# One search step for the order of a fused attention and MoE kernel: all engines, loads, paces and PSUM banks

## The chip, the core and the metric

The kernel runs on one core of one Trainium2 chip. The metric is the device time of one execution in microseconds; three runs were shown for the kernel before. TensorE is called PE, ScalarE ACT, VectorE DVE, GpSimd POOL and SyncE SP, as the profile names them.

## The reference

```python
batch, n_heads, seq, head_dim = (8, 8, 1152, 64)     # q, k, v in float32
q_pool = q.reshape(B, H, S // 2, 2, D).mean(axis=3)  # pairs of query rows are averaged
scores = scale * np.matmul(q_pool, k.transpose(0, 1, 3, 2))
attn = softmax(scores)                               # with the row's maximum and sum
x = matmul(attn, v).transpose(0, 2, 1, 3).reshape(4608, 512)
h1 = x @ w1; h2 = x @ w2                             # 512 -> 1024
out = np.maximum(h1, h2) @ w_out                     # 1024 -> 512
```

So there are 8 batches of 8 heads, 576 pooled queries against 1152 keys each, and then a two-layer block on 4608 tokens whose middle is the larger of two products.

## The kernel before, in words

**Work.** Two heads of one batch make a *pair*; there are 32 pairs. For each, SP loads q, k and v (576 KB each, three raw buffers of each kind, used in turn), POOL casts them to bf16 (q by adding its two rows), and k and q are turned so that the head dimension lies on the partitions: k by a DMA transpose from SP (`ktrans`, L475; from pair 5 on), q by eight 32x32-block transposes on DVE (`qtrans_dve`, L485). The first five pairs are turned on PE. PE makes the scores in groups of 512 columns for both heads (`scores`, L302, 324 groups, each over two PSUM banks), ACT takes their exponential to bf16 (`exps`, L317, 336 instructions), and PE multiplies with v, in which a column of ones gives the sums (`av_jobs`, L621 for 128-row chunks and L636 for the 64-row rests). DVE divides (L651, L654), and a DMA transpose from SP (L703) puts the result into `xT`.

The MoE block uses max(h1, h2) = relu(x(w1 - w2)) + x w2. POOL makes w1 - w2 once (`w_diff`), PE makes w2 times w_out once (the two w jobs), then *h jobs* (L760) give the relu part by token blocks of 128 to 512 columns (evacuated by DVE at L771 or ACT at L775), and *p jobs* (L803) add relu part times w_out and x times w2 w_out for 256 tokens (evacuated at L809 or L812, stored from SP at L829 or L835). The last tokens are three *z jobs* (L846). An h or p job runs its contraction on 64-row halves in two turns, with the halves swapped in the second; the second turn's first matmul waits for the first turn's results (`fence=True`).

**Order.** Every engine works through one list in order, and all five lists come from one string of letters: each letter issues the next piece of its kind (S scores, E an exponential, A an AV part, 0 to 3 a part of an open MoE job, 4 to 7 and 8, 9, +, - the evacuation of such a job by DVE or ACT, a an AV division step, k, q, v the casts, r a q transpose, t and x the DMA transposes, l the next load of LOADS, o and z stores, F a filler matmul). BANKS gives each opened piece its PSUM bank. Waits follow from the data that a piece reads and overwrites. So the string decides on what stands behind what on an engine, and on SP's queue in particular loads, DMA transposes and stores stand in one order.

**Pacing.** From the 40th exponential on, a load of q, k or v waits besides for the exponential that was issued two before its place in the string (`pace`):

```python
def pace():
    g = done[0] - PACE
    return [f"E{g}"] if PACE and g >= PACE_FROM else []
```

Of the kernel before, what the change touches and what calls it, by code (L numbers as in the profile page):

```python
# [116 lines left out]
def bass_funnel_attn__then__act_maxout2_kernel(  # L117
# [11 lines left out]
    E = moe_w_out.shape[1]  # L129
    SQ = S // 2  # L130
    NT = S // P
    HP = P // 2
    QU = SQ // HP
# [14 lines left out]
    K0 = (0, 2, 4, 6, 9)  # L148
# [12 lines left out]
    BEHIND = ()  # L161
    FILL = 28
    FILLS = 16
    PACE = 2
    PACE_FROM = 40
    FOUR = 1
    LOADS = (
# [14 lines left out]
    )  # L182
    MOE = (
        "wwhhhhpphhhhpphhhhhhhhpphhhhpphhhhphhhhpphhhhphhhhphhhhpphhhhhhhhhphphh"
    )
    BANKS = (
        "0124605424023623462032424660232342630240624702402064202420472042646264246024604640164604264126402406"
        "0240260240246304260346204040640606062061262062062402740264062402406402640642704260202402402406401640"
        "6460462056204620462046042164206204620620426026402602602602604604614646046046024604604204620420642040"
        "6406406742064264264206520640260462620620162062046206240620206204230642042042424126426046046045620642"  # L190
        "6024062046206206206206412640246056046206404024024026423236042642042626260262626426454526420642064206"
        "2454"
    )

    ctx = ExitStack()
    with ctx:
# [146 lines left out]
        def load_k(i, lo=0, hi=NT, eng="SP"):  # L343
            b, h0, s = i // NHP, 2 * (i % NHP), i % 3
            old, name = behind() if eng == "SP" else ([], [])
            op(eng, lambda e: e.dma_start(  # L346
                kraw[s][:, :, lo:hi, :].rearrange("p h t d -> p h (t d)"),
                k[b, h0:h0 + 2, :, :].rearrange("h (p t) d -> p h (t d)", t=NT)[
                    :, :, lo * D:hi * D]),
                after=([f"kraw0.{c}" for c in K0] if s == 0 and hi - lo == NT else []) + pace() + old,  # L350
                w=([f"kraw0.{lo}"] if hi - lo < NT else [f"kraw{s}"]) + name,
                dma=f"d_kp{lo}" if hi - lo < NT else f"d_k{s}",
                cost=0.2 * (hi - lo) + 0.03 if hi - lo < NT else 1.45 + 0.6 * (i == 1), tag=("L", "k", i))

        def load_q(i, lo=0, hi=QU, eng="SP"):
            b, h0, s = i // NHP, 2 * (i % NHP), i % 3
            old, name = behind() if eng == "SP" else ([], [])
# [5 lines left out]
                after=(["qraw0.0", "qraw0.4"] if s == 0 and hi - lo == QU else []) + pace() + old,  # L363
# [561 lines left out]
        def step(c):  # L925
# [5 lines left out]
            elif c == "E":  # L931
                g, go = exp_at.pop(0)
                go()
                done[0] = g
            elif c in lines or c in "0123":
                if c not in opened:
                    job = (moe if c in "0123" else lines[c]).pop(0)
# [19 lines left out]
                 "m": ("Z", 0), "4": ("0", 0), "5": ("1", 0), "6": ("2", 0), "7": ("3", 0),  # L957
                 "8": ("0", 1), "9": ("1", 1), "+": ("2", 1), "-": ("3", 1)}
        for c in (
            "luFFlulllfyKQklgfbSkKEFlgFKSgESyFFlKEFgQSbESlFkSFEFFKlEySFSgESlqFFEFQlSbEFkSQElbKvSEgSlESceAAEATcESA"  # L960
            "EAhlkSaSEaASclEKAEglSAEcSAElvSaTaEhElTcSAESlAhAEScAElSSAcEAAlAqESa0a00aE0la0ScAE0SldQEaa00bSd0lEXSj0"
            "00ESvTl0h0E00eS4SlEAAkAEAlSa1ad1E1S1SEl1q1S1E1Kl1g1qE1S1SE1lQkrAEbArSdtAErArSE11avlEa1S5AElSdArESSrA"
            "dArEArSAEkAlaAaSEaAdatAESaXadjXEjSjSEXq0jl00jE0S0qr0E0lSr01rE11e41Sl1E1Sk1r10Er005St0ESv00r0ESSr0rvE"
            "lA4AAEASqalSaEAArAErAlSrSEEaAeaAArxAErSSaAEaAklrAAErS1at1ak1E1r0Sr0xE0r0Sr11E1rS1r0E050Sl0E0q0SrS0tE"
            "r01r10Er0eS0r0E0r0Skr0lE0r1S0r0E0rlSv0r1E14S11El1S1oSE1oAAEASAkEAaAlaSAEtAvSa1aE1SxS11ES111E1111ES11"
            "l1ESq5AAEAlSrSoEAroArAESrkSArEAaAalAEAaAaSvaaEtaSSrXEqArAjAEAjSrle00Ea0aS0rSE0lr0vSr0E1r01rlE114S11E"
            "1S1rSEA5AlvAEASr0E0ta0Eva0SrSE00xe00SE4AAkAESSlAEAaAaAEAlSa1aE1Sx000E0Sk11E0lS11E11S50qlE00tS00ESer0"
            "0rSE00rS0rE00r00Er0l0qSrSE0r01l1r0E14S11E1l1SroSE1r1o11roSErAoArAtEkArAAaaAArq1ESaa1E1Sx001r001E1r0S"
            "1rE0l001rS141E1rS1r1ES5AAEvAAroSSrvoESAlAAEvAaAaAlEAaAkaSa000SaEt0a000011114Ee111S111115E1S111Xl5EvS"
            "j00j0ESl0qSE0000SEl4AAAEArSSaEAaArAlqEArS1a1taE11rSESrE1e1xrS1r1EA5AAEASla0kaE0Sr00rSEq0l0r0SEr0ArAl"  # L970
            "E4SAAESr11aE1a1Srx1ESr11r1SEt5qAAAEArSe0aE0a0Slr0SEkr0S0r0E0lrS0r0E0r0Sl0rE0000ES0S0Er0tArAEArArS0aE"
            "0aq0Srx10Er1S14k1E1S11EroS1rSo1E1oAAoEvAAS1vElSAAlEAvAaSa1ESalAaAAEASa1aE1taS1rXvE1rS1j11Ej1eSrl11rE"
            "11qrSS5EAlAAkEAroS0a0oEa0S0rS0ErAAlAEASa0a0E0l0S4x00E0qSE0r00E0trSA4eAEAArS1a1Ea1k1Sr11ESr1lSr1E5AAA"
            "lEArS1a1Ea11Srx00E10S1l1E1S500tE0Sq0rS0Er00r0e0ESr00rSEl0kr00r0E0rS0l0ES00SE0A4AAEAAaAoaAoASaoSqaE11"
            "x11SESkr11t1rE11rE11rE1SrS1E1r11r1SEr11S1E1S11E1A5AEvAASoSvESlAAoAEvAaAaAElAaAa0Sa0a0E0taS00r0000E04"
            "e0Sx000r0E11141vS1x1E11r100500Sr11qE1Sr01lr110E1rS050E0Sl0r0E0SS0l0E0S0r0EArAArEAArlAkaAaArSE0etEa0a"
            "S0r0SE0rxS0rq0EA4AAEASkao1aE11o1SSE11lS11EA5AAElASa1aE1Sx0r00E0rS1rt0E0er0Sr0E1S4111ESl1r0q0E500S0lE"
            "0SrS0r0EA4lAAEAAAaaAASa1aESlk1Sx1r1ES1r11Ert11r11Er1qSSr1E1rArAEvAS1E11klS11El11vS1E1S1lvA5ESAAEAoAa"
            "oSaSESaAtaArAEArq00Ea0aSa00rExSv0r00ErS0xe0r0E0rSSr0kl0E0S00E0Sl00E0S00El0A4AEAAAaoSaSEoArAtArE00Ea0"
            "0aeS00rxE1111r00qS411E1111151S1k1E1r1Sl00500ESr000SrEl0A4AAEArSla1aE1S1S1EAAAEAlSa1aE1tSrS1rq1E1r1x1"  # L980
            "1rESSre11Er11rSk1Elr11S1E11Sl1E1A5AAEASaoSaEAoAAoEAoSa0a0tEq00rSESr0E00rx00k040E0AArvAArSrSvElArArAE"
            "AvaAaAAaAaSaSaE00a001x14E11S11E1x11Sv511E100S1SE0r1t11r0ES0500E0eSr00Er00SrSE0r00r0SEr0S00E0S00E0004"
            "0E00S0E0oS00oSE4AAAEAAaAaAeAAaEAaAAxAaAaAASa0aES0x00SE1000E0S411E1S11E111500S0E00S11E1S11E1S10E50S00"
            "E0S10E0Se10E00S00E0S00E0S00E10S41E11S11EoS11o1E1oSSo1E1AAEAAAaAaAAAaAaAxAAAAAaAaAAaAa1a1a1a11X1j11j1"
            "11111900001111111150000111o080110091o110000008101110191101000018111009101110000080101111191100000001"
            "001111910000000011111111110001000800110000o008001o11o00010181111Z9ZZZZZoZZoZZZZZZmZZZZzzZZZZZZZZZZmZ"
            "ZZZZZZzZzmzz"
        ):
            step(c)
# [52 lines left out]
```

## Time and profile before

| | us |
|---|---|
| three runs | 357.15, 358.04, 360.08 |
| median | 358.04 |
| span of the profiled execution | 356.4 |
| TensorE busy | 346.0 (97%) |
| ScalarE busy | 313.8 (88%) |
| VectorE busy | 230.1 (65%) |
| GpSimd busy | 151.4 (42%) |

For the profiled execution the page gives its span alone, the time from the first to the last instruction; the median of the three runs lies 1.64 us above it. Matmuls overlap in TensorE, so sums of their durations exceed the time that they take; start-to-start distances are used where that matters. The granted TensorE clock of the profiled execution is 0.999. Lines such as L302 are those of the kernel's file.

### The profile page before, as it was taken

The page shows a single profiled execution, that of the slowest core. Times are in us where ns is not written, and L with a number is a line of the kernel's source. Part 1 is how long each engine was busy: PE and PEld are TensorE (multiplying, and loading weights), DVE is VectorE, ACT ScalarE, POOL GpSimd, SP SyncE. Part 2 cuts the span into 40 slices and gives each one's busy share as a digit, 9 for nine tenths or more (in the row PEclk, how much of TensorE's full clock was granted, in tenths as well). Part 3 has the DMA queues.
Part 4 walks back from the last instruction along what each step waited for, and adds up shares of the span by engine and source line. Part 5 has one row for each costly group of instructions (what it writes and reads, how often), then busy time and mean ns, then how long its engine had stood idle before and what let it go on. Part 6 is the DMA issues. An engine that isn't in the chain of part 4 may idle for free.

```text
span 356.4 us, 13757 instructions
## 1 busy us (share of the span) xinstructions
PE 346.0 (97%) x6178; PEld 218.5 (61%) x6178; DVE 230.1 (65%) x472; ACT 313.8 (88%) x354; POOL 151.4 (42%) x136
## 2 busy tenths in 40 slices
PE   7889999999899999999999999999999999999996
PEld 5556665656564675656666576556576757448753
DVE  2587589974966867985887677785586875414001
ACT  5999999999999899999999989989999796992431
POOL 2625997554564264355544455227444621010000
PEclk9999999999999999999999999999999999999999
DMA  8999999999989989998999699998999943012215
GB/s 271 403 397 398 370 255 309 280 289 261 293 252 279 315 196 350 237 301 183 278 320 260 153 230 301 237 314 234 224 299 255 267 68 75 17 32 47 61 31 148
DMA packets 76699, 84.55 MB, mean 237 GB/s; under 512 B 48480, under 2 KB 49760, under 8 KB 76640
## 3 DMA queue, kind: packets, MB, share of 16 engines
q1 hardware_dynamic: 75856, 83.15, 87.5%
q8 instruction: 48, 0.79, 0.9%
q10 hardware_dynamic: 784, 0.52, 0.5%
q14 instruction: 11, 0.09, 0.1%
HBM read 62.91 MB, written 9.44 MB: 203 GB/s over the span
## 4 chain that ended last, share of the span: by engine, by line
PE 87%; ACT 9%; DMA 2%; issue 1%; SPq 0%; DVE 0%
PE ps L803 25%; PE ps L621 20%; PE ps L302 19%; PE ps L760 16%; ACT et L317 9%; PE ps L636 3%; PE ps L593 2%; DMA qraw<-in_q_dram 2%; PE ps L846 1%; PE ps L552 0%; PE ps L533 0%; SPq L346 0%; DVE qp L428 0%; SPq L358 0%; PE ps L730 0%
## 5 line engine op out<-in xcount | busy, mean ns | idle before, releaser
L317 ACT ACTIVATE et<-ps 128x1024 bf16<-128x1024 f32 (+1 forms) x336 | 302.4, 1019 | 14.5 <-PE ps L302 9.7
L302 PE MATMUL ps<-qpT,kT 64*128 64x256 bf16 (+7 forms) x1162 | 117.3, 283 | 2.7 <-issue 1.1
L485 DVE STREAM_TRANSPOSE qpT<-qp 32x288 bf16<-32x288 bf16 x216 | 101.4, 469 | 10.4 <-PE ps L302 6.1
L760 PE MATMUL ps<-xT,wd 64*128 64x512 bf16 (+3 forms) x832 | 81.2, 311 | 0.2
L302 PEld LDWEIGHTS ps<-qpT,kT 64*128 64x128 bf16 x1162 | 48.3, 94 | 49.7 <-ACT et L317 11.3
L803 PE MATMUL ps<-wo,stage 64*128 64x512 bf16 x544 | 76.4, 376 | 0.0
L435 POOL TENSOR_TENSOR qp<-qraw 128x576 bf16<-128x576 f32 x30 | 42.1, 1406 | 61.1 <-DMA qraw<-in_q_dram 57.3
L621 PEld LDWEIGHTS ps<-vE,et 128*128 128x128 bf16 x1728 | 54.9, 97 | 13.9 <-ACT et L317 9.3
L621 PE MATMUL ps<-vE,et 128*128 128x65 bf16 x1728 | 60.7, 193 | 0.7 <-issue 0.3
L771 DVE TENSOR_SCALAR stage<-ps 128x1024 bf16<-128x1024 f32 (+3 forms) x41 | 39.7, 970 | 21.1 <-PE ps L760 20.6
L760 PEld LDWEIGHTS ps<-xT,wd 64*128 64x128 bf16 x832 | 35.6, 94 | 22.2 <-PE ps L760 1.9
L405 POOL TENSOR_SCALAR kbf<-kraw 128x1152 bf16<-128x1152 f32 x31 | 35.7, 1153 | 26.3 <-DMA kraw<-in_k_dram 25.6
L803 PE MATMUL ps<-w,xT 64*128 64x512 bf16 x272 | 40.8, 377 | 0.0
L803 PEld LDWEIGHTS ps<-wo,stage 64*128 64x128 bf16 x544 | 26.4, 94 | 20.5
L445 POOL TENSOR_SCALAR vE<-vraw 128x1152 bf16<-128x1152 f32 x24 | 27.4, 1154 | 19.4 <-PE ps L636 10.8
L809 DVE COPY stage<-ps 128x1024 f32<-128x1024 f32 x14 | 17.1, 1224 | 23.1 <-PE ps L803 23.0
L468 POOL TENSOR_SCALAR stage<-et 128x1152 bf16<-128x1152 bf16 x14 | 16.1, 1152 | 35.5 <-ACT et L317 35.5
L654 DVE TENSOR_TENSOR xnat<-ps,rc 128x256 bf16<-128x256 f32 (+2 forms) x71 | 27.6, 397 | 2.0
L651 DVE RECIPROCAL rc<-ps 128x4 f32<-128x4 f32 (+2 forms) x64 | 11.6, 182 | 25.9 <-PE ps L621 25.5
L621 PEld LDWEIGHTS ps<-stage,et 128*128 128x128 bf16 x576 | 18.1, 97 | 2.7 <-issue 2.6
L621 PE MATMUL ps<-stage,et 128*128 128x65 bf16 x576 | 19.7, 193 | 0.0
L803 PEld LDWEIGHTS ps<-w,xT 64*128 64x128 bf16 x272 | 12.5, 94 | 8.8 <-DVE stage L771 0.2
(55 smaller groups left out, 155.4 us busy)
## 6 DMA issues: line engine op xcount, KB each, us to landing
vraw<-in_v_dram SPq DMA_DIRECT2D x32, 576.0 KB, 6.1
kraw<-in_k_dram SPq DMA_DIRECT2D x31, 576.0 KB, 6.7
qraw<-in_q_dram SPq DMA_DIRECT2D x31, 576.0 KB, 6.3
out_dram<-stage SPq DMA_DIRECT2D x24, 256.0 KB, 4.1
out_dram<-stage SPq DMA_DIRECT2D x21, 128.0 KB, 3.4
xT<-in_moe_w_dram SPq DMA_DIRECT2D x4, 512.0 KB, 12.2
stage<-in_moe_w_out_dram SPq DMA_DIRECT2D x4, 512.0 KB, 14.1
stage<-in_moe_w_dram SPq DMA_DIRECT2D x4, 512.0 KB, 13.2
```

What stands on the lines that cost most here:

```text
L302: last = e.matmul(ps[:, h, col:col + hi - lo], kT[i % 3][rows(h), t, :], qpT[i % 3][rows(h), lo:hi], start=True, stop=True)
L317: op("ACT", lambda e: e.activation(et2[:, :, c:c + z - a], ps[:, :, a - g * W:z - g * W], EXP, scale=scale), r=[f"b{m}", f"b{m + 1}"], w=w ...
L405: op("POOL", lambda g: g.tensor_scalar(kbf[s][:, :, :, :].rearrange("p t h d -> p h t d"), kraw[r][:, :, :, :], 1.0, 1.0, ALU.mult, ALU.mu ...
L435: op("POOL", lambda g: g.tensor_tensor(qpf[s][:, :, :], qraw[r][:, :, 0, :], qraw[r][:, :, 1, :], ALU.add), r=[f"qraw{r}"], w=[f"qp{s}.0", ...
L445: return g.tensor_scalar(vE[r][:, :, :, 0:D].rearrange("p t h d -> p h t d"), vraw[s][:, :, :, :], 1.0, 1.0, ALU.mult, ALU.mult)
L485: op("DVE", lambda e: e.transpose(view[dst:dst + 32, :, 32 * pb:32 * pb + 32], qpf[s][src:src + 32, :, 32 * db:32 * db + 32]), r=[f"qp{s}. ...
L621: last = e.matmul(fb[m][:, at * 66:at * 66 + 65], et[:, a:a + P], vE[vs][:, t, half, 0:65], start=(t == 0), stop=(t == NT - 1))
L654: todo.append(evac_op("DVE", lambda e, m, z=z, at=at, num=num, dst=dst: e.tensor_tensor(dst, a(m)[z, at:at + num, 0:D], rc[k][z, at:at + n ...
L760: last = e.matmul(fb[m + k][:, 0:size], wd[z, ct, (f0 + k) * P:(f0 + k + 1) * P], xT[z, ct, n0:n1], start=(turn == 0 and ct == 0), stop=(t ...
L771: return e.tensor_scalar_max(gT[:, f0:f0 + 2, g0:g0 + size], wide[m // 2][:, :, 0:size], 0.0)
L803: last = e.matmul(fb[m + k][:, :], lhs, rhs, start=(turn == 0 and j == 0), stop=(turn == 1 and j == NC_ + NF - 1))
L809: return e.tensor_copy(osb2[:, o:o + 2, :], wide[m // 2][:, :, :])
```

## The change

The string of letters, LOADS, BANKS and the order of the MoE jobs are replaced. The number of letters of each kind stays, apart from which MoE job's stream a part belongs to and the names of the evacuations (four streams, 0 to 3, are now open near the end; there were two). PACE is replaced by PACES, a number for each load that SP issues: the exponential it waits for, or -1 for none; the weights' loads have such a number too.

```diff
-    PACE = 2
-    PACE_FROM = 40
...
-        ("q", 0, 4, 9), ("k", 1), ("q", 1), ("q", 2), ("k", 2), ("v", 0), ("w", 0, 1), ("w", 0, 3),
...
-        ("k", 29), ("v", 29), ("q", 30), ("k", 30), ("v", 30), ("q", 31), ("k", 31), ("v", 31),
+        ("q", 0, 4, 9), ("q", 1), ("k", 1), ("k", 2), ("q", 2), ("v", 0), ("w", 0, 1), ("w", 0, 3),
...
+        ("v", 27), ("k", 29), ("k", 30), ("q", 31), ("v", 30), ("v", 29), ("k", 31), ("v", 31),
+    PACES = (
+        -1, -1, -1, -1, -1, -1, -1, -1, -1, -1, -1, -1, -1, -1, 10, 9, 12, -1, 17, 13, 13, 19, 19, 23,
...
+        -1, 224, 229, 231, 233, 244, -1, 250, -1, 252, 267, 267, 259, 277, 270, 275, -1, 287, 291, -1,
+        304,
+    )
...
-        "wwhhhhpphhhhpphhhhhhhhpphhhhpphhhhphhhhpphhhhphhhhphhhhpphhhhhhhhhphphh"
+        "wwhhhhpphhhhpphhhhhhhhpphhhhpphhhphhhhhpphhhhphhhhphhhphphhhhhhhhhhhphp"
...
-        def pace():
-            g = done[0] - PACE
-            return [f"E{g}"] if PACE and g >= PACE_FROM else []
-
-        done = [0]
+        def pace(eng="SP"):
+            g = PACES[issued[0] - 1] if eng == "SP" else -1
+            return [f"E{g}"] if g >= 0 else []
+
...
-                w=[f"{key}{c}"] + name, after=old, dma=f"d_w{part}{c}", cost=1.34, tag=("L", "w", part, c))
+                w=[f"{key}{c}"] + name, after=pace() + old, dma=f"d_w{part}{c}", cost=1.34, tag=("L", "w", part, c))
...
-            "luFFlulllfyKQklgfbSkKEFlgFKSgESyFFlKEFgQSbESlFkSFEFFKlEySFSgESlqFFEFQlSbEFkSQElbKvSEgSlESceAAEATcESA"
+            "luFFlulllllylfQlfKbFlFkglSkKlFEFgKSlgylESKQgEbSySESkEFQFbESSkEKSgEFqFFESSKvEFgFEFSQEbFlSclSEAAAcElS"
...
-            "1rE0l001rS141E1rS1r1ES5AAEvAAroSSrvoESAlAAEvAaAaAlEAaAkaSa000SaEt0a000011114Ee111S111115E1S111Xl5EvS"
+            "S00oE1110S10E500rSSE0A4AAEvASoSESvAlAAEAaAaAEAlaAaSa000a0tESa00001411E00100Sl111q1E000lS504XE0jeS0j0"
...
+            "11aESa11005E0xq0S00E00So400E0011S0l0E1oS001Eo411So1E1eS111E1SS1E111SE1111E1SvS1E110v500E0S00Ero00So4"
+            "SEAlAAEArAAarAeArAEAaAaAaAAaAaASakSaE00r00rSEt0r000E14S1l1E1xS1r1E11Sx50E0111x1rS0E0S111E1S500E000S0"
...
-            "11111900001111111150000111o080110091o110000008101110191101000018111009101110000080101111191100000001"
+            "10020911012212000011228122o0000+12252o21110002120228000+11122220123923330200021816113311110393001-02"
```

The narrow (128-wide) h jobs of the third token block are the letters `000011114Ee111S111115` in the old order and `000a0tESa00001411E00100Sl111` in the new. The load of k31 is the `l` in `So4` / `SEAlAA` at the end of the new order's pieces above; the cast, `k`, and the transpose, `t`, follow further on in the same line.

More of the change, by code (lines that the diff above doesn't have):

```diff
@@ L349, in load_k @@
                     :, :, lo * D:hi * D]),
-                after=([f"kraw0.{c}" for c in K0] if s == 0 and hi - lo == NT else []) + pace() + old,
+                after=([f"kraw0.{c}" for c in K0] if s == 0 and hi - lo == NT else []) + pace(eng) + old,
                 w=([f"kraw0.{lo}"] if hi - lo < NT else [f"kraw{s}"]) + name,
@@ L362, in load_q @@
                 w=([f"qraw0.{lo}"] if hi - lo < QU else [f"qraw{s}"]) + name,
-                after=(["qraw0.0", "qraw0.4"] if s == 0 and hi - lo == QU else []) + pace() + old,
+                after=(["qraw0.0", "qraw0.4"] if s == 0 and hi - lo == QU else []) + pace(eng) + old,
                 dma=f"d_qp{lo}" if hi - lo < QU else f"d_q{s}",
@@ L970, in bass_funnel_attn__then__act_maxout2_kernel @@
[L970 to L974, printed above, removed]
@@ L985, in bass_funnel_attn__then__act_maxout2_kernel @@
[L985 to L986 removed]
+            "luFFlulllllylfQlfKbFlFkglSkKlFEFgKlSgylESKQgEbSySESkEFQFbESSkEKSgEFqFFESSKvEFgFEFSQEFbFlSclSEAAAcElS"
+            "SlETAhESaAcAkESAAEeScSElKalEglSAaElaTESvlhESTdAcESAAEhSAcAElASlSqaESaAaAaEAldc00ESQc0E00S0bE00qaSa0E"
+            "0X0j0Sv0lETSlh00l0ESq4AAElAAlSkaSlaE00rS0er0ESr000rEd0Kr00Eg0S0rSEQkAbAErSqtAEASEa0a0vE0lrS0AE4dSAEA"
@@ new lines, in bass_funnel_attn__then__act_maxout2_kernel @@
+            "rSdSrEAlArAlrEdSSaAaAEalAdaAlSEaXadjXESjjSEXv00j0jE0rSk00r0ESr1et11E1S0q1E41lS1l1ESlk500E00Svt0r0ESr"
+            "S0q0EA4AAEASaSaEArAAEASaSEreAEaAAxAEkSaSrAErAlArAESla00la0aE0kSrx11rE1S0qt0E00S41E1Sl111Er1Sr11Ev1rS"
+            "1r1E1erS1rSE11r11rE1lSrq0t0r1ES110E50lS0l0E0Sr0SErAArAEAAaSa0lESr0rAAErASrq0E0aSr00a0Ek0x0SSE0v00t00"
+            "ES0k0SE4lAAlAElvSrSoAErAlvrAAESaSaAEaAAaAEASaSaEaSrXEjAeAjAEASa0a0El0rSo0rSESlr00o0rE10t141E1S11E1r1"
+            "S5SEAAAEA0aSa0E0lr0ESoerS0Er0S0rk0EA4AAqEtASrSEAArxAEAaaS0a0aEl0v0SSE01q1l00ES0141E1S11E1lrS1xr1ESe1"
@@ new lines, in bass_funnel_attn__then__act_maxout2_kernel @@
+            "r1SrE1l1rk11r1ESSrv1t1Er11r00kEr00rS0E1rq1Sr01ES5000E00SroSEArtAArEAAkaArAlAao0EaSa0oE0rS0xr00E1r111"
+            "S00oE1110S10E500rSSE0A4AAEvASoSESvAlAAEAaAaAEAlaAaSa000a0tESa00001411E00100Sl111q1E000lS504XE0jeS0j0"
+            "Er0Sr00E0qS0SE4lAAlAEArSSrEAArAvEAaa0Sa0aE00xvS0E0ESS00EA4AAEASa0kaE00rS0rSEetS0r00Er0kA4lAESAAErlS0"
+            "al0a0E0rxSSr0E0r0t0SE4AAAqEASa0aE0Srk00r0E0rSeS0rE00r00Erq0SrS0E0r00r0E0rSSr0E0rAArAEAqSa0aE0Sx001E4"
+            "S11l1E1lSrSo1Er111rSErAArAEArSr1E1lSkAoAEAoAaSrt1vESaAaAAEaASa1atE1aS111ESv1o11EXoSe1j1E1jlSrS1EA5AA"
@@ new lines, in bass_funnel_attn__then__act_maxout2_kernel @@
+            "EASa0a0E0l0rSSr0EArAAEAlSla0a0E0l114lS1k1ESE111SeE1lA5oAAEAxrS0q0aE0a0Sl00Et00S4SEAAlrAEAoSa0a0E00rS"
+            "Sr0E00r1q11E014S1E1v1SrS1Er11kr11ESr11vrtSE1r11r1eES1rx11rE1qSrS1lrE1ArAA5EAAkAAaoAaSr0E00rS0r0ES0tr"
+            "0k0E0r0ESa0aE0oSrS0ro0E00lS0E00S0E0000ES4AAEAAroSSESlAxAAEAaAaAEAlaAaSa00aE00aS00rx001E11e41S111E1x0"
+            "00q0S09001l0E14Sv11E1r00Sr00E1vlrS00lr001Et14S11Er11rSl1E111S1ESAAAEAqAaArAArSEr1E1k1aS1aa1E1vSt1SE5"
+            "AAkAElASla0eaE00rS0rSESr000rE0A4AEAASa0aE11S1t1ES111E1So500E0lSq0l0Er00S40eE000S0rE0Sr0S0ErAAAEAAaAa"
```

37 lines of the change are left out of this document (12 added, 25 removed), and 25 rows, old and new, of tables (LOADS, PACES).

## The prediction

> **What bounds the kernel now.** I read the page first: the span, the busy shares, the slices and the first line of the chain.
>
> ```profile
> span 356.4 us, 13757 instructions
> PE 346.0 (97%) x6178; PEld 218.5 (61%) x6178; DVE 230.1 (65%) x472; ACT 313.8 (88%) x354; POOL 151.4 (42%) x136
> ...
> PE   7889999999899999999999999999999999999996
> ...
> ACT  5999999999999899999999989989999796992431
> ...
> PEclk9999999999999999999999999999999999999999
> ...
> PE 87%; ACT 9%; DMA 2%; issue 1%; SPq 0%; DVE 0%
> ```
>
> TensorE is busy for 97% of the span at full granted clock, and 87% of the chain is TensorE's; ScalarE has 9% of it. To see where each of the two rules, I cut the span into three stretches and the end.
>
> ```profile
> 0.00:60.00 60.00, 54.30 (x1032) 33.70 (x1032) 40.14 (x76) 55.10 (x63) 37.88 (x42) 1.00 1.02 345
> 60.00:100.00 40.00, 38.74 (x706) 24.72 (x707) 30.91 (x68) 39.40 (x45) 20.10 (x18) 1.00 1.06 286
> 100.00:340.00 240.00, 239.72 (x4324) 152.91 (x4322) 158.04 (x328) 215.63 (x244) 93.46 (x78) 1.00 0.86 212
> ```
>
> ```profile
> 18.00:36.00 18.00, 16.22 (x355) 10.25 (x357) 14.68 (x24) 17.60 (x21) 7.42 (x7) 1.00 1.04 397
> ...
> 340.00:356.40 16.40, 13.23 (x126) 7.17 (x122) 0.98 (x2) 3.70 (x5) 0.00 (x0) 0.98 0.38 97
> ```
>
> After the length the columns are PE, PEld, DVE, ACT, POOL. From 100 to 340 us TensorE idles 0.28 us of 240 while ScalarE has 24 us to spare: TensorE alone rules. Up to 100 it is the other way: ScalarE runs 39.40 of 40 us between 60 and 100, and its idle time before 60, 4.9 us, is nearly all ahead of its first exponentials. This is where that start is set:
>
> ```profile
> 2.24 0.47 SPq L358 DMA_DIRECT2D qraw<-in_q_dram  x1
> ...
> 6.08 2.85 ACT L317 ACTIVATE et<-ps 128x1024 bf16<-128x1024 f32 x3 [0.91 <-PE ps L552]
> ...
> 8.17 0.49 DVE L428 TENSOR_TENSOR qp<-qraw 128x320 bf16<-128x320 f32 x1 [1.25 <-DMA qraw<-in_q_dram]
> ...
> 9.43 3.77 ACT L317 ACTIVATE et<-ps 128x1024 bf16<-128x1024 f32 x4 [0.49 <-PE ps L302]
> ```
>
> Three exponentials run on the first part of q; the fourth, at 9.43, follows the second part, whose load is the fourth of SP's list, is issued at 2.24 and is added up at 8.17. From there ScalarE goes on almost without a gap until TensorE takes over near 100 us.
>
> **The change part by part.** It adds and removes no instruction: the letters of the two orders have the same number of scores, AV parts, MoE parts, casts, transposes, loads and stores, and 14 evacuations stay on ScalarE. So the sum is made of waits and of costs that hang on neighbours.
>
> *Start-up.* The first four loads of SP keep their place, so the fourth exponential still starts at about 9.43. k1 and q1 change places, as do k2 and q2; each is one 576 KB load behind its old place and is wanted by the scores of its pair only. Before the hundredth exponential both orders issue the same TensorE work (98 scores, 76 AV parts, 39 and 48 MoE parts). I count this at 0. Bound: all ScalarE idle time that is left from 9.43 to 100 (0.49, then 0.40 from 18 to 36, and 0.60 from 60 to 100), 1.5 us to gain; to lose, a second pair of gaps like the 0.91 and 0.49 above, 1.4 us, if k1 comes too late.
>
> *Changes of tile shape.* Between 128-row AV matmuls and 64-row pairs TensorE loses time:
>
> ```profile
> 298.09 4.45 PE ps L621 x144
> ```
>
> ```profile
> 93.46 1.26 PE L621 MATMUL ps<-vE,et 128*128 128x65 bf16 x36
> 94.65 0.39 PE L302 MATMUL ps<-qpT,kT 64*128 64x256 bf16 x4
> ```
>
> 144 in a row take 4.45 us, 0.0309 each, so 36 want 1.11; from 93.46 to the next start at 94.65 are 1.19. One change costs some 0.1 us. Counting letters of neighbours, I get 172 changes before and 160 after. But 11 of the 12 lie ahead of the hundredth exponential, where ScalarE's time covers them (39.40 of 40); without that cover they would be 1.1 us. On the path is 1: 0.1 us gained.
>
> *Drains inside narrow h jobs.* The second half of an h job swaps its row halves and waits for the first half's results (the fence). In the 128-wide block the old order has nothing in between:
>
> ```profile
> 130.86 0.33 PE L760 MATMUL ps<-xT,wd 64*128 64x128 bf16 x6
> 131.03 0.38 PE L302 MATMUL ps<-qpT,kT 64*128 64x384 bf16 x4
> 131.24 1.32 PE L760 MATMUL ps<-xT,wd 64*128 64x128 bf16 x24
> 132.40 0.38 PE L302 MATMUL ps<-qpT,kT 64*128 64x448 bf16 x4
> 132.61 0.74 PE L760 MATMUL ps<-xT,wd 64*128 64x128 bf16 x12
> 133.19 0.38 PE L302 MATMUL ps<-qpT,kT 64*128 64x512 bf16 x2
> ```
>
> Six narrow matmuls take 0.17 us to the next start, 0.028 each. The 24 from 131.24 should be through in 0.68 and take 1.16; the 12 from 132.61 should take 0.34 and take 0.58. That is 0.48 + 0.24 = 0.72 us in three drains. In the new order another job's parts or scores stand in all of these places. This is in TensorE's own stretch, so all of it counts: 0.7 gained, at least 0.5 if one part is too short a cover.
>
> *The one long stall.*
>
> ```profile
> q8 instruction: 48, 0.79, 0.9%
> ```
>
> ```profile
> 92.70 0.61 PE L302 MATMUL ps<-qpT,kT 64*128 64x128 bf16 x8 [1.12 <-issue]
> ```
>
> For 1.12 us TensorE waited for nothing that the profile shows. No letter of the order explains it, so I leave it in: 0, at most 1.1 gained. [...]
>
> *Paces and late loads.* The old rule held every load behind the exponential two before its place; now each has a number of its own, 29 of 110 have none, and the weights' later loads are paced too. On SP's queue the stores, DMA transposes and loads are in one order, and many loads now stand later. The tightest is the last pair: k31 now stands behind the two stores at 296.98 (which wait for an evacuation), and only then come its cast and transpose, which the first scores of pair 31 need at 311.18. Before, it was issued at 272.57 and transposed at 288.96.
>
> ```profile
> 272.57 0.37 SPq L346 DMA_DIRECT2D kraw<-in_k_dram  x1
> ...
> 288.96 1.29 SPq L475 DMA_TRANSPOSE kT<-kbf  x1
> 296.98 1.32 SPq L829 DMA_DIRECT2D out_dram<-stage  x2
> ...
> 311.18 0.38 PE L302 MATMUL ps<-qpT,kT 64*128 64x448 bf16 x4
> ```
>
> ```profile
> L405 POOL TENSOR_SCALAR kbf<-kraw x24: 1150/1152/1159, 64.7 to 279.3; 128x1152 bf16<-128x1152 f32 x24
> ...
> DMA to landing us min/median/max: 4.3/6.3/8.1
> ```
>
> ```profile
> DMA to landing us min/median/max: 4.4/5.1/6.9
> ```
>
> The first landing row is that of kraw loads from 60 to 290 us, the second of kT transposes from 268 to 312. So k31 can be issued at 296.98 + 1.32 = 298.30. With the medians it is in place at 298.30 + 6.3 + 1.15 + 5.1 = 310.85, 0.3 us early; with the quickest at 308.15, 3.0 early; with the slowest at 314.35, 3.2 late. I take 0, because that late stretch has far less traffic than the one that the median comes from. [...] Behind a late kT the whole of TensorE's queue stands, and ScalarE and VectorE wait for that.
>
> *The end.* MoE jobs are now taken in up to four bank pairs at a time rather than two, with the last z jobs in the same order. TensorE has no gap to fill there until its last matmul (the 3.2 us of idle time in 340 to 356.4 are the last evacuation and store, which are the same). 0, with 0.5 either way for an evacuation that comes early or late.
>
> **Sum.** 356.4 - 0.1 - 0.7 = 355.6 us of span. The shown runs have their median, 358.04, 1.64 above the profiled span; that stays, so 357.2 us, 0.2% faster than before.
>
> **The rivals.** *A: the keys come too late.* One mechanism: loads and transposes near the end have lost their lead, and a transfer of ordinary slowness holds TensorE. Place: kT of pair 31 (7 exponentials now between the transpose's place and its first scores, 21 before), then of 29 and 27 (7 and 8 now, about 20 before). Price: 3.2 us for pair 31 with the slowest rows, and up to 1 for each of the other two. 357.2 + 3.2 + 1.6 = 362.0. It decides from the point where load, cast and transpose together exceed 311.18 - 298.30 = 12.9 us. For it: the median path is 12.55. Against it: the quiet queue, and that a store or two issued earlier gives the time back.
>
> *B: little late ends eat the gain.* The last of a pair's eight q transposes on VectorE now stands at most three exponentials ahead of the scores that need it in pairs 15, 19, 24 and 30 (five to seventeen before).
>
> ```profile
> L485 DVE STREAM_TRANSPOSE qpT<-qp 32x288 bf16<-32x288 bf16 x216 | 101.4, 469 | 10.4 <-PE ps L302 6.1 <-POOL qp L435 0.8
> ```
>
> One transpose late by its own length costs 0.469; four cost 1.9: 357.2 + 1.9 = 359.1. For it: the old order left the scores far behind. Against: VectorE is 65% busy and has an evacuation at most in front.
>
> *C: clearly faster.* If every gap goes, 0.8 + 1.5 (ScalarE before 100) + 0.6 (what of the 1.12 is not in that) + 0.3 (TensorE from 100 to 340) = 3.2, 354.8; with some of the 1.64 us that runs have over this profile, 353.5. Against it: the fixed fourth load, and a TensorE stretch with 0.28 us of idle time.
>
> *D: the new paces do nothing*, because no transfer ends a TensorE wait after 100 us. Then drains and the changed shape are all that is left, which is the forecast's own number.
>
> **How the numbers follow.** Forecast with D 0.47 (its own range 355.1 to 358.4), B 0.24, A 0.21, C 0.08. A change of 1% (3.6 us) is about what a measurement of this kernel can tell from no change. Faster than 354.5 needs C: 0.08. Slower than 361.6 needs A: 0.21. Between: 0.71. The range reaches from C's 354.6 or so to just short of A's: 354.6 to 361.9.
>
> **What would show it.** Right: no drains left in the 128-wide L760 rows; ScalarE's fourth exponential still near 9.4; TensorE idle under 1 us from 100 to 340; the last kT landing before its scores. Wrong: waits of L302 for kT or L485, or of POOL's last casts for kraw followed by a TensorE gap; a ScalarE gap between 10 and 60 us; a granted clock below full anywhere but at the end.

## The result, and the profile after

The changed kernel takes 361.36 us (median of 12 runs, 360.73 to 362.65); the kernel before, on the same chip, 359.34 (12 runs, 356.96 to 361.40). The ratio is 1.0076 with a 95% interval of 1.0050 to 1.0101. A second comparison of the same two kernels gave 1.0069 (1.0026 to 1.0112). So the change costs 2.0 to 2.7 us; the prediction had 0.8 us gained. That 361.36 lies inside the predicted range (354.6 to 361.9) is luck: the chip of this comparison ran the kernel before in 359.34, 1.3 us above the median that the prediction started from, and the slow end of the range came from rival A, whose late keys did not occur (below).

The page of the changed kernel, the first lines, the two blocks of TensorE's and the loads' queue, and the chain:

```profile
span 359.7 us, 13731 instructions
...
PE 346.9 (96%) x6178; PEld 218.3 (61%) x6178; DVE 229.8 (64%) x472; ACT 313.9 (87%) x354; POOL 150.9 (42%) x136
...
q8 instruction: 48, 0.79, 0.9%
...
PE 88%; ACT 9%; issue 1%; DVE 0%
```

TensorE's work is the same to 0.9 us (346.9 against 346.0), and so is its instruction count; the span is 3.3 us longer (359.7 against 356.4). The windows say where it lies (columns as in the prediction: length, then PE, PEld, DVE, ACT, POOL, the granted clock, the DMA engines' busy share, GB/s):

```profile
0.00:60.00 60.00, 51.37 (x1004) 32.87 (x1004) 37.82 (x74) 52.59 (x60) 36.41 (x41) 1.00 1.02 340
60.00:100.00 40.00, 39.82 (x718) 24.55 (x714) 29.82 (x65) 39.84 (x45) 19.94 (x17) 1.00 1.08 286
100.00:340.00 240.00, 239.13 (x4320) 152.70 (x4316) 159.28 (x331) 219.32 (x248) 94.60 (x79) 1.00 0.88 213
```

ScalarE ruled the first 60 us before, and it now works 52.59 of them instead of 55.10: 2.5 us are lost there. From 100 to 340 TensorE idles 0.87 us instead of 0.28. The waits put down to `issue` (idle us, how many, longest), and the timeline around the two longest, show what it is:

```profile
PEld ps L626 <- issue: 10.1, 28, 1.7
PE ps L626 <- issue: 3.4, 4, 1.6
```

```profile
28.22 0.66 PE L626 MATMUL ps<-vE,et 128*128 128x65 bf16 x16
30.18 0.51 PE L626 MATMUL ps<-vE,et 128*128 128x65 bf16 x11 [1.31 <-issue]
30.62 0.82 PE L308 MATMUL ps<-qpT,kT 64*128 64x448 bf16 x8
31.05 1.02 ACT L323 ACTIVATE et<-ps 128x1024 bf16<-128x1024 f32 x1 [1.49 <-PE ps L308]
...
49.30 0.54 PE L626 MATMUL ps<-stage,et 128*128 128x65 bf16 x12
51.40 0.61 PE L626 MATMUL ps<-stage,et 128*128 128x65 bf16 x15 [1.56 <-issue]
51.94 0.61 PE L308 MATMUL ps<-qpT,kT 64*128 64x64 bf16 x8
52.37 1.02 ACT L323 ACTIVATE et<-ps 128x1024 bf16<-128x1024 f32 x1 [1.21 <-PE ps L308]
```

Twice TensorE stops in the middle of a row of equal AV matmuls, waits for nothing, and goes on; the scores behind it are late and ScalarE stands for 1.49 and 1.21 us. It is the stall that the prediction saw once, at 92.70 in the kernel before, and left alone.

**What these stalls are.** The q8 row fits TensorE's program: 48 packets in 0.79 MB, 16 KB each, for the 12,422 instructions that TensorE's queue has in the trace (12,356 matmuls and weight loads, 66 semaphore instructions and drains between them; 12,417 in the old order). I numbered all of these in the order of their starts from 0 and looked at every pause between two starts of more than 0.7 us from 18 to 338 us, in all profiles of this study but those of the three kernels whose loads were held back (below): 23 of 26 end at number 256k + 449 exactly, whatever instruction stands there, in both orders, and TensorE goes on 1.2 to 1.9 us after the end of packet k of q8 (also from 0). In the changed kernel, packet 2 ends at 28.80 and TensorE goes on at 30.18; packet 5 ends at 49.85 and TensorE goes on at 51.40. (The other three are one and the same wait near 21.5 us, in the old order.) Numbered without the semaphore instructions, the places no longer lie 256 apart (952 and 1715 for the two long pauses of the changed kernel, 763 apart and not 768). My reading of these numbers, which no row of a trace shows directly: TensorE has used up what it holds, and the next block of its program is late. I call this theory S; the sum of these pauses is from now on "the stalls" (those near 0.2 us and more counted, where the same place has no such pause in the other profiles of its order).

| profile | stalls, us (at) | sum | span | span less stalls |
|---|---|---|---|---|
| before | 0.54 (28.5), 1.47 (91.2) | 2.0 | 356.4 | 354.4 |
| after | 1.49 (28.7), 1.75 (49.6), 0.50 (285), three of 0.2 to 0.4 | 4.65 | 359.7 | 355.1 |

2.6 of the 3.3 us are these stalls. (The 4.85 and 354.9 in the expectations below are reached with one more pause of 0.21 us; those of that length stand at the same places in the kernel with a third of the data too, so they are no stalls.) The new order has lost the one at 91 and has got a longer one at 28.7, a new one at 49.6 and several small ones.

### The profile page after: what moved, and what is told of

The parts are those of the page before. It is cut to its first block, busy times and chain, and to the rows that moved or that the text cites. A ratio compares the mean times of both kernels' runs of the same rounds, so it can differ in the third digit from the quotient of the medians.

```text
span 359.7 us, 13731 instructions
## 1 busy us (share of the span) xinstructions
PE 346.9 (96%) x6178; PEld 218.3 (61%) x6178; DVE 229.8 (64%) x472; ACT 313.9 (87%) x354; POOL 150.9 (42%) x136
## 4 chain that ended last, share of the span: by engine, by line
PE 88%; ACT 9%; issue 1%; DVE 0%
PE ps L808 24%; PE ps L626 20%; PE ps L308 19%; PE ps L765 17%; ACT et L323 9%; PE ps L641 2%; PE ps L598 2%; PE ps L851 1%; PE ps L520 1%; PE ps L557 1%; PE ps L538 0%; DVE stage L776 0%; DVE xnat L659 0%; PE ps L735 0%; DVE stage L856 0%
## 5 line engine op out<-in xcount | busy, mean ns | idle before, releaser
L308 PE MATMUL ps<-qpT,kT 64*128 64x256 bf16 (+7 forms) x1162 | 115.4, 283 | 2.2 <-ACT et L323 1.5
L808 PE MATMUL ps<-wo,stage 64*128 64x512 bf16 x544 | 75.6, 376 | 0.0
L776 DVE TENSOR_SCALAR stage<-ps 128x1024 bf16<-128x1024 f32 (+3 forms) x40 | 38.2, 957 | 42.4 <-PE ps L765 41.8
L808 PE MATMUL ps<-w,xT 64*128 64x512 bf16 x272 | 39.4, 377 | 0.0
L814 DVE COPY stage<-ps 128x1024 f32<-128x1024 f32 x15 | 18.4, 1224 | 25.2 <-PE ps L808 25.2
L656 DVE RECIPROCAL rc<-ps 128x4 f32<-128x4 f32 (+2 forms) x64 | 11.7, 182 | 28.5 <-PE ps L626 28.4
```

The costliest lines, as they stand in the source:

```text
L308: last = e.matmul(ps[:, h, col:col + hi - lo], kT[i % 3][rows(h), t, :], qpT[i % 3][rows(h), lo:hi], start=True, stop=True)
L776: return e.tensor_scalar_max(gT[:, f0:f0 + 2, g0:g0 + size], wide[m // 2][:, :, 0:size], 0.0)
L808: last = e.matmul(fb[m + k][:, :], lhs, rhs, start=(turn == 0 and j == 0), stop=(turn == 1 and j == NC_ + NF - 1))
L814: return e.tensor_copy(osb2[:, o:o + 2, :], wide[m // 2][:, :, :])
```

## The experiments

In all of them "new" is the changed kernel's order and "old" the one before; ratios are to the kernel before on the same chip.

**The same number of instructions in other places: fillers.** The 16 filler jobs (letter F) hold two matmuls each. One less or one more in each moves the count of all that follows by 32 (a matmul and its weight load, 16 times); the starting fillers likewise.

```diff
-            return Job(("f", n), 1, [(["rem0"], 0.0563 * 2, "f", False, lambda e, m: fill(e, m, 2))], [])
+            return Job(("f", n), 1, [(["rem0"], 0.0563 * 2, "f", False, lambda e, m: fill(e, m, 1))], [])
```

*New order, one matmul.* 

> The new order with one matmul instead of two in each of the 16 fillers of the start-up: 32 TensorE instructions fewer ahead of everything else. Theory S (TensorE runs out of instructions: a 16 KB block of its program, on the instruction queue q8, lands late behind the data, and the blocks end at fixed places of the instruction stream): every block end moves 32 instructions later in the order; laid over the profile of the new order this leaves some 1.4 us of such gaps of 4.7 us, so about 358.5 us, 3 us less than the 361.4 of the new order. Theory D (the gaps in the AV parts at 28.5 and 49.6 us are late data or divisions that the profile doesn't name): the same gaps at the same AV parts, 361 us within 0.7.

Measured: ratio 1.0039 (1.0015 to 1.0062), 359.95 us; stalls 1.11 and 1.03, sum 2.1, span less stalls 354.7. By its ratio the time fits theory D (361 to 359.34 is 1.0046) better than S (358.5 would be 0.9977); the places decide. (The profile is of the quickest of the 12 runs, 358.55.) The pauses are now before scores, no longer among AV matmuls:

```profile
30.31 0.60 PE L308 MATMUL ps<-qpT,kT 64*128 64x512 bf16 x3 [0.74 <-issue]
...
50.41 0.59 PE L308 MATMUL ps<-qpT,kT 64*128 64x64 bf16 x7 [0.83 <-issue]
```

*Old order, one matmul.* 

> The old order with one matmul instead of two in each filler. Theory S: the gaps of 1.5 us at 91 us and 0.5 us at 28.5 us move off the AV parts; about 0.6 us of such gaps stay, so 1 to 1.5 us faster than the old order, some 358.0 us. Theory D: no change, 359.3 us within 0.7.

Measured: 1.0040 (1.0015 to 1.0065), so slower and not faster. The stall near 28 grew from 0.54 to 1.60, the one near 91 went to 93.8 and to another line (1.13), and 0.42 at 285.1 is new. Off the AV parts as expected at one place of two; the size is not.

*New order, three matmuls* (`fill(e, m, 3)`). 

> The new order with three matmuls in each filler: 32 TensorE instructions more. Theory S: the gaps move 32 instructions earlier in the order and sum to some 5.0 us instead of 4.7, in other places (one of them new, near 171 us): 361.4 to 362.5 us. Theory D: the same gaps at the same AV parts, 361.4 to 362 us. It tells the two apart by the places.

Measured: 1.0031 (1.0006 to 1.0056), 359.65 us: the two long stalls are gone and others came, 0.98 at 283.6, 0.79 at 169.4, 0.50, 0.31, 0.21; sum 2.8. Not the 361.4 us or more that both theories had; the places speak for S.

*New order, 12 starting fillers for 28* (`FILL = 12`). 

> The new order with 12 instead of 28 matmuls in the first filler, so again 32 TensorE instructions fewer, but taken from the time before any data has landed. Theory S: as with the shorter fillers, about 358.5 us, or up to 1 us more if TensorE's clock starts slow. Theory D, or a theory that the fillers themselves take time from the start-up: 361 us or more.

Measured: 1.0075 (1.0045 to 1.0105), stalls 1.10 and 1.03 and three of 0.4 to 0.5, sum 3.4. It is the same shift as with one matmul in each filler, and the two long stalls are the same (1.11 and 1.03 there); the time is that of the changed kernel: a miss for the expected size.

Together: the count decides at which instruction TensorE stops, exactly, and how long it then stands was not to be had from another run's packets.

**A third of the data.** From pair 3 on, each load of k, q and v brings only the first three of nine tiles; the rest of the buffer keeps old data, so the outputs of those pairs are not the reference's. Every TensorE instruction stays.

```diff
+        def thin(i, hi):
+            return hi if i < 3 else 3
...
-                kraw[s][:, :, lo:hi, :].rearrange("p h t d -> p h (t d)"),
+                kraw[s][:, :, lo:thin(i, hi), :].rearrange("p h t d -> p h (t d)"),
```

*New.* 

> The new order, but from pair 3 on each load of q, k and v brings only a third of its data (the rest of the buffer keeps older data, so the output is not the reference's); no instruction and no wait is added or removed. Theory S: with short queues the blocks of instructions land early, no gap of over 0.25 us is left at a block end after 60 us, and the span comes to 354.9 us less what is left of gaps at the start, so about 356.5 us in all. Theory D2 (the two orders differ in waits between engines, and late instructions are a side show): the new order stays 2 us or more above the old one with the same thin loads.

*Old.* 

> The old order with the same thin loads from pair 3 on (output not the reference's). Theory S: 354.4 us of span without its gaps, about 356.1 us in all, within 0.8 us of the new order with thin loads. Theory D2: 2 us or more below the new order with thin loads.

Measured: new 357.55 us, 0.9973 (0.9953 to 0.9993); old 357.68 us, 0.9964 (0.9941 to 0.9988). The changed order, 0.76% slower with its data, is level with the old one when two thirds of them are left out. Theory D2's 2 us between them are not there. In the old order no stall is left; the new one has none behind 60 us, as S had it, and keeps 1.08 at 28.4 and 0.30 at 23.0, where its weights and first pairs still load. Both kernels are 1.0 and 1.6 us slower than S had put them. In the profiles their level is a sum of two things: the old one has its fifth exponential 1.4 us later than the new one's (11.24 against 9.83; its clock record shows full speed only from 10.5 us, against 5.8), about what the new one's stalls cost. Behind them, from the 31st exponential to the last, the two differ by 0.4 us. In which of the other runs the start was late is not shown; three of the ten old ones took 356.5 us, the rest 357.4 to 358.6. The new order with a third of the loads, the same windows as above:

```profile
0.00:60.00 60.00, 53.34 (x1028) 33.90 (x1030) 39.95 (x77) 54.48 (x62) 38.46 (x43) 1.00 0.80 258
60.00:100.00 40.00, 39.84 (x722) 24.48 (x719) 29.76 (x64) 39.85 (x45) 17.88 (x15) 1.00 0.56 136
100.00:340.00 240.00, 239.66 (x4330) 153.23 (x4328) 157.12 (x329) 216.82 (x246) 94.42 (x79) 1.00 0.53 116
```

The trace does not show when TensorE asks for a block, so I measure from instruction 256k + 200 to the start of the block's packet (a few packets start before it). The mean of the blocks from 100 to 300 us is 0.6 us here and 2.29 in the changed kernel, 0.5 and 1.84 in the old order: this is what the data do. Compared exponential by exponential, the distance between the two thin kernels stays between -0.1 and +0.25 us from the 101st to the 166th, and is 0.01 at its start and -0.05 at its end: in that stretch the prediction had saved 0.7 us of drains.

**No paces.** New: `pace()` returns nothing. Old: `PACE = 0`.

*New.* 

> The new order with no load waiting for an exponential any more (order, data and buffers as they are). Theory S: more loads stand in the queues, the blocks of instructions start later in the stretch from 45 to 300 us, and gaps at block ends grow: 362 to 365 us. Theory L (loads come too late in the new order): earlier loads cannot hurt, 359 to 361.4 us.

*Old.* 

> The old order with its pacing switched off. Theory S: as in the new order, deeper queues and later blocks from 45 us on, 360 to 363 us, 1 to 4 us above the old order. Theory L: no change, 358.5 us within 0.7.

Measured: new 359.52 us, 1.0032 (1.0013 to 1.0051); old 358.21, 0.9990 (0.9965 to 1.0015). Theory S as I had put it, that paces keep the queues short and blocks early, missed both. The new order's paces do the reverse: without them its stalls are 2.6 instead of 4.65, and the one at 49.6 is gone. In the old order the paces make no difference beyond the interval.

**Which paces?** Early ones are those of SP's first 41 loads (issued before about 65 us).

```diff
-            g = PACES[issued[0] - 1] if eng == "SP" else -1
+            g = PACES[issued[0] - 1] if eng == "SP" and issued[0] <= 41 else -1
```

*Early paces alone.* 

> The new order with its paces for the first 41 of SP's loads alone (those that fall ahead of about 65 us), the later loads unpaced. Without any pace it was 0.44% faster than with all. Theory S: the early paces put loads of 576 KB and weights into the time of the blocks k2 and k5, so the stall near 50 us stays (1 us or more) and those behind 100 us shrink: 360.5 to 361.4. Rival L: the late paces cost nothing, since no transfer is late there, and the time is that of the changed kernel, 361.4; both agree in sign, and only the places of the stalls tell more.

*Late paces alone* (`issued[0] > 41`). 

> The new order with paces for the loads from the 42nd on alone. Theory S: the stall near 50 us is under 0.6, as without any pace, those behind 100 us sum to 1 to 1.6 us as in the changed kernel: 359.5 to 360.5. Rival (paces matter by the lead of the data alone): 359.5, as without paces.

Measured: early alone 360.72 us, 1.0054 (1.0025 to 1.0083), stalls 1.51 at 28.3 and 0.41 at 49.3 besides small ones; late alone 359.31, 1.0022 (0.9995 to 1.0049), stalls 1.62 at 28.2, 0.52 at 282.7, and 0.18 near 49. The time with early paces is as expected by S (and by rival L), the one with late paces just below S's 359.5; the stall near 50 is smaller than expected with the early paces, and with the late ones those behind 100 us sum to 0.5 and not to 1 to 1.6. Both profiles are of the quickest run of their kernel (358.56 with early paces, 2.2 below the median), so these stalls may be low draws. It was 0.4 to 2.6 us in six of the seven profiles with the early paces and all their data (none with fillers of three matmuls), and 0 and 0.18 in the two without. SP's list and a window around it (its last column GB/s), in the changed kernel:

```profile
43.90 1.38 SPq L480 DMA_TRANSPOSE kT<-kbf  x1
45.33 4.39 SPq L351 DMA_DIRECT2D kraw<-in_k_dram  x2
```

```profile
48.00:51.00 3.00, 1.84 (x47) 1.23 (x44) 2.46 (x5) 3.00 (x4) 3.00 (x4) 1.00 1.08 74
```

Late paces alone:

```profile
42.91 1.34 SPq L480 DMA_TRANSPOSE kT<-kbf  x1
44.30 1.11 SPq L351 DMA_DIRECT2D kraw<-in_k_dram  x2
```

```profile
48.00:51.00 3.00, 3.00 (x70) 2.04 (x65) 2.87 (x8) 3.00 (x5) 3.00 (x3) 1.00 0.75 259
```

With the paces the transpose is issued 1 us later, the issuing of the two loads of k behind it takes 4.4 us instead of 1.1, and from 48 to 51 us the DMA engines, at a full busy share, move only 74 GB/s; block 5's packet starts at 47.1 and takes 2.7 us instead of 1.1. (In the repeat of the changed kernel, below, it takes 1.1 but starts only at 49.2.) Without the early paces that slow spell lies earlier, from 46 to 49 us, and then is over. That the slow spell comes from the transpose and the loads together is argued, not shown.

**The count shifted within the same starting time.** 60 starting fillers of 59 columns for 28 of 128 in the old order (64 more instructions), 48 of 74 in the new (40 more). Places and sizes had been worked out from the packets of the earlier profiles.

```diff
-                op("PE", lambda e: fill(e, 7, FILL), r=["rem0"], w=["b7"], cost=0.0563 * FILL, mode="f",
+                op("PE", lambda e: fill(e, 7, FILL, 59), r=["rem0"], w=["b7"], cost=1.58, mode="f",
```

*Old.* 

> The old order; the 28 filler matmuls at the very start become 60 of 59 columns (3540 columns in all instead of 3584), so every later instruction of TensorE stands 64 places further on and nothing else changes. Theory S (instruction blocks arrive late and stop TensorE at index 256k+449): the stalls of the profile before, 0.54 at 28.5 and 1.47 at 91.2 us, sit on other code, where TensorE reaches the index later against the block's arrival; worked out from the fetch delays of the two profiles of the old order, the sum of such stalls is 0.7 to 1.4 us instead of 2.0, so the kernel is 0.5 to 1.3 us faster than before (ratio 0.9965 to 0.9985) and the stall near 91 us is gone or under 0.8. Rival L (the time belongs to the order of transfers and paces): the same time as before, stalls at the same places in time.

*New.* 

> The new order; the 28 starting fillers become 48 of 74 columns, 40 places more. Theory S: by the fetch delays of the changed kernel's own profile this is the worst place within reach: the sum of stalls at index 256k+449 goes from 4.85 to between 6 and 9 us, the kernel is 1 to 4 us slower than the changed one (362.4 to 365.4; ratio to before 1.010 to 1.019). Rival L: 361.4, ratio 1.0076, as the changed kernel, with stalls at the same times.

Measured: old 360.01 us, 1.0033 (1.0005 to 1.0061). The stall at 91 went, as S said, and the sum fell to 1.0; the time still rose. In the profile the start came 1.45 us later (sixteenth exponential at 21.74 instead of 20.29), with matmuls at half speed: the clock record begins full speed at 13.4 us, against 4.2 in the kernel before, and six fillers of 128 columns take 0.82 us at 11.76 and 0.51 at 14.24. Whether the other runs started so late is not shown. Four score matmuls of 256 columns take 0.60 us in the shifted kernel and 0.39 in the kernel before (second fence):

```profile
1.12 3.61 PE L515 MATMUL ps<-rem 128*128 128x59 bf16 x64 [1.12 <-DVE rem L399]
...
5.91 0.60 PE L302 MATMUL ps<-qpT,kT 64*128 64x256 bf16 x4 [0.39 <-DVE qpT L540]
```

```profile
5.65 0.39 PE L302 MATMUL ps<-qpT,kT 64*128 64x256 bf16 x4 [0.39 <-DVE qpT L540]
```

New: 360.14 us, 1.0026 (0.9997 to 1.0055), not the 362 to 365 expected: the stalls went to other places (0.83 at 27.7, 0.71 at 47.6, 1.25 at 168.9, 1.14 at 264.2), and their sum is 3.9 us, below the changed kernel's. From one profile the sizes could not be forecast.

**Loads held back.** From SP's 15th load on, each waits for the landing of the third (or second) load before it.

```diff
-    BEHIND = ()
+    BEHIND = ((14, 3),)
```

*New, three.* 

> The new order with its paces; from SP's 15th load on, each load waits besides until the load three before it has landed (in the profile of the changed kernel that delays 59 loads, by 0.2 to 5.1 us, mostly ahead of 60 us and around 91 to 99 us). Theory Q (a block waits behind the data in flight): its packet starts earlier after TensorE asks for it (mean from index 200, 45 to 100 us: 2.93 in the changed kernel, under 2.2 here), the stalls at index 449 sum to less than 2.5 us, ratio to before 0.998 to 1.004. Rival B (the engines are busy whatever is in flight, and only the bytes matter, as with the loads cut to a third): delays, stalls and time as in the changed kernel, 1.006 to 1.010. Rival K (loads become late): exponentials or TensorE wait for kraw, vraw or qraw, over 1.010.

*New, two.* 

> As new_flight3 with two instead of three. Theory Q: stalls below 1.5 us in sum, ratio 0.995 to 1.001, unless data come late. Rival B: as the changed kernel. Rival K: over 1.010, and more than new_flight3.

*Old, three.* 

> The old order with the same cap of three (in its profile that delays 24 loads, by 7 to 11 us ahead of 35 us, where up to twelve are in flight, and by 0.6 to 3.6 around 79 to 99 us). Theory Q: the stall near 28 us (0.54) goes, the one near 91 us (1.47) shrinks below 0.8, ratio to before 0.995 to 0.999. Rival B: 1.000. Rival K: a weight or a pair's data late ahead of 60 us, over 1.003.

Measured: 365.14 us, 1.0174 (1.0133 to 1.0216); 381.32, 1.0621 (1.0565 to 1.0676); 365.36, 1.0181 (1.0138 to 1.0225). Rival K holds: the data come late. (In the old order the stall near 28 us went, as Q had it, and the one near 91 is 0.97 at 97.4, not below 0.8.) The new order with three, casts and TensorE waiting for loads:

```profile
39.33 1.15 POOL L450 TENSOR_SCALAR vE<-vraw 128x1152 bf16<-128x1152 f32 x1 [1.34 <-DMA vraw<-in_v_dram]
40.62 1.24 PE L626 MATMUL ps<-vE,et 128*128 128x65 bf16 x36 [1.22 <-POOL vE L450]
42.23 9.34 ACT L323 ACTIVATE et<-ps 128x1024 bf16<-128x1024 f32 x11 [1.46 <-PE ps L308]
```

With three the blocks came no earlier (mean wait from 45 to 100 us 2.83, against 2.93 without a cap; in the old order 2.68 against 1.90), so theory Q, loads in flight alone, is not borne out there. With two the mean is 1.40 and the stalls sum to 1.2, as Q had it, but TensorE then stands for data (3.8 us before 58.5), so it asks for blocks more slowly too, and the run does not decide.

**Once more.**

*The changed kernel.* 

> The changed kernel once more, nothing edited. If the stalls' places come from the instruction count, they are again at index 256k+449; their sum is between 2 and 5 us (4.85 the first time; 2.1 to 3.4 in the variants of the new order), the span less these stalls 354.7 to 355.1, and the ratio to before 1.004 to 1.010. If 4.85 was the rule and not a high draw, the sum is again above 4.

*The kernel before.* 

> The kernel before once more, nothing edited. Ratio 1.000 within its interval. If places come from the instruction count, the stalls are again at index 449 of block 2 (near 28 us) and block 11 (near 91 us) and nowhere else above 0.3 us; their sum is 1 to 3 us, the rest of the span 354 to 356.5, with up to 1 us of scatter in the start of the fifth exponential (9.7 to 11.4 us in the profiles of the old order so far).

Measured: the changed kernel 1.0069 (1.0026 to 1.0112), stalls 1.25 at 28.8, 2.59 at 49.5, 0.54 at 284.7, sum 4.4; the kernel before 0.9996 (0.9958 to 1.0033), stalls 0.67 at 28.0 and 2.29 at 91.1, sum 3.0. The long ones are at the same places as in their first profiles. So the new order has 4.4 to 4.65 us of stalls and the old one 2.0 to 3.0, 1.4 to 2.6 us apart, beside medians that are 2.0 to 2.7 apart.

One expectation failed: the span less stalls of the repeated changed kernel is 356.6, not 354.7 to 355.1. Over all profiles without held loads it is 354.4 to 356.6 in the new order and 353.9 to 356.5 in the old. The highest, 355.5 to 356.6, are the five in which TensorE's clock record has 3.4 us at half speed on the way, or full speed only from 10 us or later; the others lie between 353.9 and 355.3. So what the stalls leave over is level within about 1 us, not closer.

## Why the prediction was wrong, point by point

**The step that failed is "The one long stall", entered as 0, at most 1.1 gained.** Its sentence "No letter of the order explains it" was wrong: an order fixes which instruction is number 256k + 449, and with its loads when TensorE gets there and how late the block is. The order and its paces move these stalls, and a stall can appear as well as go. In place of "0, at most 1.1 gained" the runs show 1.4 to 2.6 us lost by stalls. Measured, as the growth of the distance between the same exponentials of the two profiles: the stall at 28 is longer, +1.2 us from the 26th to the 31st; the one at 49.6 is new, +1.3 from the 46th to the 61st; the one at 91 is gone, -0.9 from the 91st to the 101st; and +1.6 from there to the end, where the small ones lie. The stalls themselves grew by 2.6 us (table). The prediction also had no rival that ends slower by this mechanism; A, the slowest, looked at the data's transfers and B at VectorE's transposes. Its list of signs did have the one that came, a ScalarE gap between 10 and 60 us (1.49 at 31.05 and 1.21 at 52.37), but no mechanism for it. On the page the clue was there: the q8 row beside a wait on `issue`.

Of the 47 instructions numbered 256k + 449 in the changed kernel 41 show no stall; the six others cost 4.65 us of 360, beside transfers at 213 to 340 GB/s (the windows above). That most of them cost nothing is no reason to leave them out of a sum.

**Changes of tile shape (−0.1)** and **drains in narrow h jobs (−0.7)**: not seen. Counted in the traces, the changes of shape fall from 160 to 148, by 12 as predicted, but 10 of the 12 lie ahead of the hundredth exponential and not 11, so that term would have been 0.2. The drains of the 128-wide block are gone, but at one of their places TensorE now waits for an exponential:

```profile
133.79 0.57 PE L765 MATMUL ps<-xT,wd 64*128 64x128 bf16 x14
134.57 0.45 PE L765 MATMUL ps<-xT,wd 64*128 64x128 bf16 x10 [0.21 <-ACT et L323]
134.86 0.38 PE L308 MATMUL ps<-qpT,kT 64*128 64x448 bf16 x4
135.07 0.56 PE L765 MATMUL ps<-xT,wd 64*128 64x128 bf16 x14
```

The 14 matmuls at 133.79 should be through in 0.39 (0.028 each, the prediction's figure) and the next starts 0.78 later. From the 101st to the 166th exponential, the stretch with these jobs, the new order takes 59.00 us in three profiles without a stall there (no paces, late paces, thin), and the old one 59.02 to 59.16 in its six without held loads: some 0.1 gained of the 0.7. Where the rest went, beyond the wait above, is open.

**Start-up (0)** holds: the first exponential at 6.41 (6.08 before) and the fifth 0.2 us earlier, at 10.13; single profiles without held loads have the fifth between 9.4 and 10.2 in the new order and between 9.7 and 11.4 in the old, the two latest with the clock at half speed up to 10.5 and 13.4 us.

**Paces and late loads (0; rival A).** Nothing late there. k31's load, cast and transpose against its scores:

```profile
301.49 0.69 SPq L351 DMA_DIRECT2D kraw<-in_k_dram  x1
307.34 1.15 POOL L410 TENSOR_SCALAR kbf<-kraw 128x1152 bf16<-128x1152 f32 x1 [3.29 <-DMA kraw<-in_k_dram]
308.51 1.34 SPq L480 DMA_TRANSPOSE kT<-kbf  x1
314.81 0.35 PE L308 MATMUL ps<-qpT,kT 64*128 64x448 bf16 x2
```

```profile
kT<-kbf SPq DMA_TRANSPOSE x1, 2.9
```

Landed at 308.51 + 2.9 = 311.4, 3.4 us early; from the load's issue it took 9.9 us, as with the quickest rows that the prediction had (the DMA engines moved 109 GB/s from 298 to 312 us, 249 from 60 to 290). (Its slowest rows add up to 314.45, 0.1 more than it says.) **Rival B**: the last q transposes of pairs 15, 19, 24 and 30 end 0.9, 1.1, 2.5 and 0.3 us before their scores; no TensorE pause follows one. **Rival D**, that the paces do nothing: the runs speak against it, with 1.0076 and 1.0069 for the new order with its paces, 1.0032 without, and stalls of 4.4 to 4.65 against 2.6. Since no data were late with the paces, I read their cost as one on the instruction queue.

What stays open: why block 2 is later in the new order (0.8 to 1.6 us of stall near 28 us in nine of its ten profiles without held loads; in the old order 0.4 to 0.7 in four, 1.6 in one, none with thin loads); whether SP's transpose or the bunched loads make the slow spell at 48 us; and how a size follows from the traffic. No version of these orders beat both kernels with its data: the old order without paces is level (0.9990, 0.9965 to 1.0015).

## What to carry to other kernels

When TensorE's profile shows pauses on `issue` and a row like q8 beside them, number that engine's instructions and see whether the pauses lie a fixed count apart, as they did here (multiples of 256). Then they are part of the schedule, and a new order can move them, here from 28.5 and 91.2 us to 28.7 and 49.6. Count every instruction of the queue, the semaphore ones too (66 of the 12,422). A sum that has engines and data alone can come out better for an order that is worse on the chip, as here (0.8 us gained, 2.0 to 2.7 lost), because the sum has no term for how late the packets of q8 start (mean 2.29 us after 256k + 200 in the new order with all its data, 0.6 with a third of the loads). To see what such stalls cost, cut the loads' bytes and keep the instructions, and compare the starts of the two profiles before calling them level.

## What the runs showed of the hardware that I had not expected

Of the 26 pauses of more than 0.7 us, 23 end at exactly instruction 256k + 449 of TensorE's queue, in both orders. A block's packet took 0.88 to 1.20 us for 44 of the 48 blocks of the changed kernel, and started up to 4.84 us after TensorE had passed 256k + 200 (4.68 in the kernel before); from 100 to 300 us the mean was 2.29 and 1.84, against 0.6 and 0.5 with the thin loads.

After the two longest of these pauses, 2.40 and 1.94 us idle, the granted clock fell to half. The second profile of the changed kernel, the pause at 49.5, and then windows of 1 us after it (the granted clock is the third column from the end):

```profile
52.12 0.98 PE L626 MATMUL ps<-stage,et 128*128 128x65 bf16 x15 [2.40 <-issue]
```

```profile
52.00:53.00 1.00, 0.88 (x15) 0.82 (x14) 0.00 (x0) 0.00 (x0) 1.00 (x2) 0.50 1.09 406
...
54.00:55.00 1.00, 1.00 (x21) 1.00 (x20) 0.40 (x1) 1.00 (x2) 0.12 (x1) 0.50 1.02 403
55.00:56.00 1.00, 1.00 (x26) 0.94 (x25) 0.10 (x1) 0.62 (x1) 0.78 (x1) 0.81 1.09 420
```

The second profile of the kernel before did the same at 93.9 us after 1.94 us of pause, with 0.50 from 95 to 97; the changed kernel's first, with 1.56, kept 1.00 (the rows at 51.40). By the clock record of both, 3.4 us of half speed lie behind each of the two. That a pause of some length brings them is not shown: the profile with fillers of three matmuls has a mean clock of 0.995 too, and no stall above 0.98 us. From the 46th to the 61st exponential in the one and from the 91st to the 101st in the other, the time grew against the first profiles by 1.4 us more than the longer stall explains. Of the changed kernel's twelve runs, three had a mean granted clock of 0.991 to 0.995; their median is 362.33, that of the other nine 361.04. No run with thin loads was below 0.998.
